# Splitting the first weight load by partitions, and four one-row copies for the result, in a decode kernel

## The chip, the cores and the metric

The kernel runs on one core of a Trainium2 chip. The metric is the time of one execution on the device, in microseconds. The kernel before was run three times: 203.63, 205.05 and 206.72 us, median 205.05. The profile was taken of an execution of 206.72 us, whose span from the first to the last instruction is 205.4 us.

## The reference

One token of a transformer block: LayerNorm, attention of 32 heads over a cache of 4096 keys and values, a residual, LayerNorm, a gated feed-forward with GELU, and a residual. All arrays are bf16.

```python
D, Hq, Sk, Dh, Df = 640, 32, 4096, 128, 1728
xn = layernorm(x)                                   # x: (1, 1, 640)
q = (xn @ wq).reshape(1, 1, 32, 128).transpose(0, 2, 1, 3)
scores = einsum("bhqd,bhkd->bhqk", q, k_cache) * Dh ** -0.5
o = einsum("bhqk,bhkd->bhqd", softmax(scores), v_cache)
h = x + o.transpose(0, 2, 1, 3).reshape(1, 1, 4096) @ wo
g, u = layernorm(h) @ w_gate, layernorm(h) @ w_up
return h + (gelu(g) * u) @ w_down
```

The inputs come to 84 MB, of which the two caches are 67 MB. Each is read once.

## The kernel before, in words

The program is written out by hand for five instruction queues: `sync` (SP, which issues nearly all DMAs), `gpsimd`, `vector`, `tensor` and `scalar`. A small class `Prog` collects operations per queue in program order, with the events that each one waits for, and `emit` writes them out with one semaphore per engine and one per DMA. `emit({"sync": 2})` places the first two operations of SP ahead of the barrier with which the program starts, so that they are issued before the other engines begin; the rest follows after it. Line 51 of the profile is the helper through which every DMA goes.

The loads form one long stream on SP's queue. First comes `wq` (L169), 640 x 4096, as one DMA into the SBUF tile `arena`: 128 partitions, on each five rows of the matrix, 40,960 bytes. Then come the caches in groups of four heads, `K` and `V` in turn (K0, V0, K1, K2, V1, K3, V2, ...), each 4 MB into one of three buffers `slot0` to `slot2` as 128 partitions of 32,768 bytes. `issue` sends the load of a slot when the group that held it has been consumed, so SP waits between loads on VectorE (for K) or TensorE (for V). After the last V group come `wo`, in three DMAs into `arena`, and then `w_gate`, `w_up` and `w_down` in several pieces into the slots.

The first use of `wq` is `q_proj` (L259), 40 matmuls that wait for the LayerNorm of x and for all of `wq`. Its result is copied to `qb` by VectorE (L263) and ScalarE (L264). For each K group VectorE multiplies the keys by q (L273), TensorE folds the products with an identity matrix (L281), VectorE reduces (L288), ScalarE takes the exponentials (L292), and TensorE multiplies by V (L310). In the feed-forward part `glu` (L417) forms gate and up, and `down` (L447) the last product.

`down` accumulates into four rows of one PSUM bank, `ps_d`, at partitions 0, 32, 64 and 96, 160 columns each, on top of the residual that four matmuls put there (L426). The last piece of `w_down` feeds one matmul for each quarter, `dn[0]` to `dn[3]`. Then ScalarE copies partitions 0 to 32 and VectorE partitions 64 to 96 into `out_row` (L460, L461), and one DMA stores rows 0, 32, 64 and 96 of `out_row` to the output.

Of the kernel before, what the change touches and what calls it, by code (L numbers as in the profile page):

```python
# [6 lines left out]
BF16 = mybir.dt.bfloat16  # L7
# [4 lines left out]
D = 640  # L12
# [89 lines left out]
def bass_sequential_preLN__gqa_block_cached__glu_gated_geglu__decode_kernel(nc, A_x, A_k_cache, A_v_cache, A_wq, A_wo, B_x, B_w_gate, B_w_up, B_w_down, out):  # L102
    sb = lambda name, shape, dt: nc.alloc_sbuf_tensor(name, shape, dt)
    SLOT = 10 * DF
    slots = [sb("slot%d" % i, [128, SLOT], BF16) for i in range(NSLOT)]
    arena = sb("arena", [128, 5 * 4096], BF16)
# [4 lines left out]
    RS = sb("RS", [128, H, 4], FP32)  # L111
    RT = sb("RT", [128, H], FP32)
    x_row = sb("x_row", [1, D], BF16)
    out_row = sb("out_row", [128, 160], BF16)
    xx = sb("xx", [128, 10], FP32)
    ln = sb("ln", [128, 8], FP32)
    xlnB = sb("xlnB", [128, 5, 32], BF16)
# [33 lines left out]
    ps_d = bank[3][:, 256:416]  # L151
# [8 lines left out]
    P = Prog(nc)  # L160
    V = lambda fn, *d: P.op("vector", fn, *d)
    A = lambda fn, *d: P.op("scalar", fn, *d)
    T = lambda fn, *d: P.op("tensor", fn, *d)
# [2 lines left out]

    A(lambda e: e.preload_act_table_set("natural_log_exp_and_others"))
    d_x = P.dma("scalar", x_row[:, :], A_x[0, :, :])
    d_wq = [P.dma("sync", arena[:, :], A_wq[:, :].rearrange("(p c) n -> p (c n)", c=5))]  # L169
    order = [("K", 0), ("V", 0), ("K", 1)]  # L170
    for G in range(1, NG - 1):
        order += [("K", G + 1), ("V", G)]
# [190 lines left out]
    for kind, G in order:  # L363
# [7 lines left out]
        if G == 4:  # L371
# [19 lines left out]
    d_wd = [P.dma("sync", wd_sb[:, 12, :], B_w_down[1536:1664, :], free[1]),  # L391
            P.dma("sync", wd_sb[:, 13, 0:320], B_w_down[1664:1728, :].rearrange("f (s n) -> (f s) n", s=2))]
# [49 lines left out]
    def down(ms, qs=range(4)):  # L442
        def fn(e):
            for m in ms:
                for q in qs:
                    h, n = (hm[:, m:m + 1], 160 * q) if m < 13 else (hm2[:, q // 2:q // 2 + 1], 160 * (q % 2))
                    i = e.matmul(ps_d[32 * q:32 * q + 1, 0:160], h, wd_sb[:, m, n:n + 160],  # L447
                                 start=False, stop=(m == 11))
            return i
        return fn  # L450
# [5 lines left out]
    T(down([13]), h2, d_wd[1])  # L456
    T(down(range(4, 8)), d_wd[3])
    T(down(range(8, 11)), d_wd[4])
    dn = {q: T(down([11], [q]), d_wd[5]) for q in range(4)}
    os = [A(lambda e: e.copy(out_row[0:33, :], ps_d[0:33, 0:160]), dn[1]),  # L460
          V(lambda e: e.tensor_copy(out_row[64:97, :], ps_d[64:97, 0:160]), dn[3])]  # L461
    d_out = P.dma("sync", out[0, :, :].rearrange("o (q n) -> (o q) n", q=4), out_row[::32, :], *os)
    P.op("sync", None, d_out)

    P.emit({"sync": 2})


# [26 lines left out]
```

## Time and profile before

| | before |
|---|---|
| median of three runs | 205.05 us (203.63 to 206.72) |
| profiled execution | 206.72 us, span 205.4 us |
| TensorE busy (matmul) | 118.7 us, 58% |
| VectorE busy | 100.8 us, 49% |
| ScalarE busy | 60.8 us, 30% |
| bytes read | 84.23 MB, 410 GB/s over the span |
| wq, issue to landing | 15.7 us |
| a K group, issue to landing (median of 8) | 21.9 us |
| mean granted TensorE clock | 0.838 |

The page cuts the span into 40 slices of about 5.1 us; a digit is the busy share of an engine in a slice in tenths. DMA is the mean busy share of 16 DMA engines. A line of the chain gives start, length and what ran, of the work that ended last. A line of the timeline gives start, length, engine, line, operation, tiles and shapes, and in brackets the idle time before it with what ended it. A line of the windows gives, after the stretch and its length, the busy time and instruction counts of TensorE's matmuls, its weight loads, VectorE, ScalarE and GpSimd, then the clock, the DMA share and the rate.

### The profile page before, as it was taken

The page shows a single profiled execution, that of the slowest core. Times are in us where ns is not written, and L with a number is a line of the kernel's source. Part 1 is how long each engine was busy: PE and PEld are TensorE (multiplying, and loading weights), DVE is VectorE, ACT ScalarE, POOL GpSimd, SP SyncE. Part 2 cuts the span into 40 slices and gives each one's busy share as a digit, 9 for nine tenths or more (in the row PEclk, how much of TensorE's full clock was granted, in tenths as well). Part 3 has the DMA queues.
Part 4 walks back from the last instruction along what each step waited for, and adds up shares of the span by engine and source line. Part 5 has one row for each costly group of instructions (what it writes and reads, how often), then busy time and mean ns, then how long its engine had stood idle before and what let it go on. Part 6 is the DMA issues. An engine that isn't in the chain of part 4 may idle for free.

```text
span 205.4 us, 2503 instructions
## 1 busy us (share of the span) xinstructions
PE 118.7 (58%) x1010; PEld 58.5 (28%) x1010; DVE 100.8 (49%) x105; ACT 60.8 (30%) x272; POOL 5.0 (2%) x14
## 2 busy tenths in 40 slices
PE   0107059438549777830957198539835787267494
PEld 0103023113213242410314033213322253167383
DVE  3201088427977869603791587187708940100221
ACT  2101005610662563630056136403640561100100
POOL 7100000000000000000000000000000000000000
PEclk9999758996985999996699969966996999955555
DMA  9999999999999999999999999999999999999970
GB/s 335 423 429 440 408 421 466 440 405 421 442 460 415 408 361 421 460 423 415 440 434 440 418 440 429 440 428 421 434 450 408 415 424 431 414 430 417 410 302 15
DMA packets 4341, 84.39 MB, mean 411 GB/s; under 512 B 489, under 2 KB 874, under 8 KB 1514
## 3 DMA queue, kind: packets, MB, share of 16 engines
q1 hardware_dynamic: 4328, 84.23, 96.4%
q8 instruction: 8, 0.13, 0.3%
q14 instruction: 3, 0.02, 0.0%
q10 hardware_dynamic: 2, 0.00, 0.0%
HBM read 84.23 MB, written 0.00 MB: 410 GB/s over the span
## 4 chain that ended last, share of the span: by engine, by line
DMA 63%; PE 17%; DVE 13%; issue 3%; SPq 3%
DMA slot<-in_A_k_cache_dram 41%; PE bank L281 12%; DVE prod L273 11%; DMA slot<-in_B_w_down_dram 11%; DMA slot<-in_A_v_cache_dram 11%; PE bank L310 3%; SPq L51 3%; DVE sc L288 1%; PE bank L319 1%; PE bank L447 0%; DVE out_row L461 0%; PE bank L330 0%; DVE RT L329 0%
## 5 line engine op out<-in xcount | busy, mean ns | idle before, releaser
L281 PE MATMUL bank<-prod,id_b 128*128 128x512 bf16 x256 | 73.5, 446 | 54.0 <-DVE prod L273 54.0
L273 DVE TENSOR_TENSOR prod<-slot,qb 128x4096 bf16<-128x4096 bf16 x32 | 72.4, 2284 | 33.8 <-DMA slot<-in_A_k_cache_dram 33.8
L292 ACT ACTIVATE p_bd<-sc,zero_t 32x32 bf16<-32x32 f32 x128 | 46.4, 362 | 87.7 <-DVE sc L288 86.5
L281 PEld LDWEIGHTS bank<-prod,id_b 128*128 128x128 bf16 x256 | 26.5, 112 | 101.1 <-DVE prod L273 66.6
L288 DVE TENSOR_REDUCE sc<-bank 128x32 f32<-128x512 f32 x32 | 22.0, 687 | 20.1 <-PE bank L281 20.1
L292 ACT ACTIVATION_READ_ACCUMULATOR p_bd<-sc,zero_t 32x1 f32 x128 | 23.5, 184 | 0.0
L310 PE MATMUL bank<-slot,p_bd 128*16 128x512 bf16 x256 | 17.3, 380 | 3.4 <-ACT p_bd L292 2.5
L310 PEld LDWEIGHTS bank<-slot,p_bd 128*16 128x16 bf16 x256 | 9.4, 89 | 7.6 <-ACT p_bd L292 3.0
L348 PE MATMUL bank<-aP,arena 128*128 128x1 bf16 x160 | 6.7, 178 | 5.3 <-DMA arena<-in_A_wo_dram 5.3
L319 PE MATMUL bank<-po_sb,hs 128*16 128x128 f32 x64 | 8.4, 274 | 1.1 <-ACT po_sb L314 1.1
L417 PE MATMUL bank<-hlnT,slot 128*128 128x1 bf16 (+1 forms) x140 | 6.7, 176 | 3.0 <-DMA slot<-in_B_w_gate_dram 3.0
L259 PE MATMUL bank<-arena,xlnB 128*32 128x512 bf16 x40 | 4.0, 578 | 7.3 <-DMA arena<-in_A_wq_dram 7.3
L348 PEld LDWEIGHTS bank<-aP,arena 128*128 128x128 bf16 x160 | 6.6, 131 | 5.5 <-DMA arena<-in_A_wo_dram 4.1
L314 ACT COPY po_sb<-bank 128x512 f32<-128x512 f32 x8 | 4.7, 585 | 9.9 <-PE bank L310 9.9
L417 PEld LDWEIGHTS bank<-hlnT,slot 128*128 128x128 bf16 (+1 forms) x140 | 6.3, 118 | 3.9 <-DVE hX L407 3.1
L244 ACT ACTIVATE ln<-ln,eps_t 128x1 f32<-128x1 f32 x2 | 0.6, 294 | 22.0 <-DVE ln L242 22.0
L319 PEld LDWEIGHTS bank<-po_sb,hs 128*16 128x16 f32 x64 | 5.6, 96 | 4.4 <-issue 2.1
L404 DVE TENSOR_TENSOR hT<-xx,bank 128x5 f32<-128x5 f32 x1 | 0.2, 161 | 11.7 <-PE bank L348 11.7
L263 DVE CAST qb<-bank 128x512 bf16<-128x512 f32 x1 | 0.7, 692 | 9.7 <-PE bank L259 9.7
L233 PE MATMUL bank<-one_bf,x_row 1*128 1x1 bf16 x5 | 0.4, 177 | 7.1 <-DMA x_row<-in_A_x_dram 7.1
L259 PEld LDWEIGHTS bank<-arena,xlnB 128*32 128x32 bf16 x40 | 1.6, 138 | 9.3 <-issue 9.3
L334 DVE TENSOR_SCALAR aT<-bank,rz 16x128 bf16<-16x128 f32 x2 | 0.7, 339 | 6.3 <-PE bank L319 6.3
(65 smaller groups left out, 25.7 us busy)
## 6 DMA issues: line engine op xcount, KB each, us to landing
slot<-in_A_k_cache_dram SPq DMA_DIRECT2D x8, 4096.0 KB, 21.9
slot<-in_A_v_cache_dram SPq DMA_DIRECT2D x7, 4096.0 KB, 18.1
arena<-in_A_wq_dram SPq DMA_DIRECT2D x1, 5120.0 KB, 15.7
slot<-in_A_v_cache_dram SPq DMA_DIRECT2D x2, 2048.0 KB, 19.9
arena<-in_A_wo_dram SPq DMA_DIRECT2D x1, 2560.0 KB, 29.0
slot<-in_B_w_gate_dram SPq DMA_DIRECT2D x1, 2160.0 KB, 17.1
arena<-in_A_wo_dram SPq DMA_DIRECT2D x1, 1920.0 KB, 33.1
slot<-in_B_w_up_dram SPq DMA_DIRECT2D x1, 1296.0 KB, 19.7
```

The source lines that it names most:

```text
L51: ev = self.op(eng, lambda e: e.dma_start(out, in_), *deps, dma=True)
L259: i = e.matmul(ps_q[hf][32 * j:32 * j + 32, :], xlnB[:, c, :], wq_j[:, c, j, 4 * hf:4 * hf + 4, :], start=(c == 0), stop=(c == 4))
L263: qa = V(lambda e: e.tensor_copy(qb[:, 0:4, :].rearrange("p g d -> p (g d)"), ps_q[0][:, :]), qd)
L273: m = V(lambda e: e.tensor_tensor(out=prod[:, s % 4, :, :], in0=kt[:, 32 * u:32 * u + 32, :], in1=qb[:, G, :].unsqueeze(1).to_broadcast([1 ...
L281: i = e.matmul(ps_f[s % 2][:, :], id_b[:, :], prod[:, s % 4, :, 16 * b:16 * b + 16], start=(b == 0), stop=(b == 7))
L288: reds[s] = V(lambda e: e.reduce_sum(sc[:, s % 4, :], ps_f[s % 2][:, :].rearrange("p (g d) -> p g d", d=16), axis=AX.X), folds[s], exps.ge ...
L292: x = A(lambda e, j=j: e.activation(p_bd[32 * j:32 * j + 32, G % 2, 32 * (s % 4):32 * (s % 4) + 32, j], sc[32 * j:32 * j + 32, s % 4, :], ...
L310: i = e.matmul(po[a:a + 16, :], p_bd[:, G % 2, 4 * b:4 * b + 4, :].rearrange("p g j -> p (g j)"), vt[:, 4 * b:4 * b + 4, :], start=(b < 4) ...
L314: evs[G] = A(lambda e: e.copy(po_sb[:, G % 2, :], po[:, :]), pvs[G], hds.get(G - 2))
L319: i = e.matmul(ps_a[0:16, 128 * (G // 4):128 * (G // 4) + 128], hs[:, r, 12 - 4 * g:28 - 4 * g], po_sb[:, G % 2, 128 * r:128 * r + 128], s ...
L348: r = e.matmul(ps_p[:, c:c + 1], wo_sb[:, t, i, c::5], aP[:, t, i:i + 1], start=(t == 0 and c == 0 and i == 0), stop=(t == 1 and i == 15), ...
L417: i = e.matmul(ps[0:128 if m < 13 else 64, m:m + 1], ws, hlnT[:, c:c + 1], start=(c == 0 and m == 0), stop=(c == 4), skip_group_check=True)
```

## The change

The load of `wq` becomes two DMAs, of partitions 0 to 15 and of partitions 16 to 127, with the same bytes in the same places. `q_proj` waits for both. Three operations of SP stand ahead of the starting barrier in place of two, so that both pieces and K0 do.

At the end, `out_row` is one row of 640 in place of 160 columns on 128 partitions. The last four matmuls run in the order of quarters 0, 2, 1, 3. VectorE copies quarters 0 and 1 and ScalarE quarters 2 and 3, one row of 160 each, and the store is one row of 640. All else keeps its place on its engine; line numbers behind the change are one higher up to the last matmuls.

```diff
-    out_row = sb("out_row", [128, 160], BF16)
+    out_row = sb("out_row", [1, D], BF16)
...
-    d_wq = [P.dma("sync", arena[:, :], A_wq[:, :].rearrange("(p c) n -> p (c n)", c=5))]
+    wq_v = A_wq[:, :].rearrange("(p c) n -> p (c n)", c=5)
+    d_wq = [P.dma("sync", arena[lo:hi, :], wq_v[lo:hi, :]) for lo, hi in ((0, 16), (16, 128))]
...
-    dn = {q: T(down([11], [q]), d_wd[5]) for q in range(4)}
-    os = [A(lambda e: e.copy(out_row[0:33, :], ps_d[0:33, 0:160]), dn[1]),
-          V(lambda e: e.tensor_copy(out_row[64:97, :], ps_d[64:97, 0:160]), dn[3])]
-    d_out = P.dma("sync", out[0, :, :].rearrange("o (q n) -> (o q) n", q=4), out_row[::32, :], *os)
+    dn = {q: T(down([11], [q]), d_wd[5]) for q in (0, 2, 1, 3)}
+    os = [V(lambda e, q=q: e.tensor_copy(out_row[0:1, 160 * q:160 * q + 160], ps_d[32 * q:32 * q + 1, 0:160]), dn[q])
+          for q in range(2)]
+    os += [A(lambda e, q=q: e.copy(out_row[0:1, 160 * q:160 * q + 160], ps_d[32 * q:32 * q + 1, 0:160]), dn[q])
+           for q in range(2, 4)]
+    d_out = P.dma("sync", out[0, :, :], out_row[:, :], *os)
     P.op("sync", None, d_out)
...
-    P.emit({"sync": 2})
+    P.emit({"sync": 3})
```

## The prediction

> **What bounds the kernel now.** I read the page's slices first, then the DMA queues, the chain of work that ended last, windows over the first and the last microseconds, and the timeline of the end.
>
> ```profile
> DVE  3201088427977869603791587187708940100221
> DMA  9999999999999999999999999999999999999970
> GB/s 335 423 429 440 408 421 466 440 405 421 442 460 415 408 361 421 460 423 415 440 434 440 418 440 429 440 428 421 434 450 408 415 424 431 414 430 417 410 302 15
> ...
> q1 hardware_dynamic: 4328, 84.23, 96.4%
> ```
>
> The 16 DMA engines are full in 38 of 40 slices; no compute engine is. The queue line gives the price of a byte: 84.23 MB in 96.4% of 16 x 205.4 us is 26.6 GB/s for one DMA engine. A row of wq on one partition is 5 x 4096 bf16, 40,960 bytes, so it takes one engine 1.54 us, and the 128 rows over 16 engines take eight such turns, 12.3 us.
>
> The chain says the same (start, length, what):
>
> ```profile
> 1.64 43.14 DMA slot<-in_A_k_cache_dram
> ...
> 75.24 20.37 DMA slot<-in_A_k_cache_dram
> ...
> 112.88 21.58 DMA slot<-in_A_k_cache_dram
> ...
> 151.24 22.15 DMA slot<-in_A_v_cache_dram
> ...
> 180.28 22.17 DMA slot<-in_B_w_down_dram
> ...
> 203.27 0.33 DVE out_row L461
> ```
>
> Only 44.8 to 75.2 us is compute. The queue serves wq, K0, V0 and K1 in order before K1 lands at 44.78, so whatever delays wq delays everything.
>
> The windows show how the stream starts and dies out (length, busy us and instruction counts of five engines, TensorE clock, DMA share, GB/s):
>
> ```profile
> 0.00:5.00 5.00, 0.00 (x0) 0.00 (x0) 1.61 (x8) 1.28 (x1) 3.87 (x12) 1.00 0.91 328
> 5.00:10.00 5.00, 0.96 (x7) 0.77 (x7) 1.33 (x6) 0.59 (x2) 1.15 (x3) 1.00 1.04 451
> ...
> 198.50:199.00 0.50, 0.50 (x14) 0.48 (x13) 0.00 (x0) 0.00 (x0) 0.00 (x0) 0.50 0.57 225
> 199.00:199.50 0.50, 0.50 (x14) 0.49 (x14) 0.00 (x0) 0.00 (x0) 0.00 (x0) 0.50 0.38 149
> 199.50:200.00 0.50, 0.50 (x14) 0.47 (x13) 0.00 (x0) 0.00 (x0) 0.00 (x0) 0.50 0.22 87
> 200.00:200.50 0.50, 0.42 (x10) 0.32 (x7) 0.00 (x0) 0.00 (x0) 0.00 (x0) 0.50 0.12 49
> 200.50:202.30 1.80, 1.55 (x41) 1.26 (x41) 0.33 (x2) 0.00 (x0) 0.00 (x0) 0.50 0.06 26
> ```
>
> A share of 0.06 is one engine of 16: from 200.5 us a single laggard finishes, while half of the engines were done by about 199 (share 0.57, then 0.38). The laggard ends at 202.4, so a typical other engine may come about 3.4 us later at no cost.
>
> The end, from the timeline:
>
> ```profile
> 202.88 0.09 PEld L447 LDWEIGHTS bank<-slot,hm 128*1 128x1 bf16 x4 [0.16 <-DMA slot<-in_B_w_down_dram]
> 203.23 0.29 ACT L460 CAST out_row<-bank 33x160 bf16<-33x160 f32 x1 [5.58 <-PE bank L447]
> 203.27 0.33 DVE L461 CAST out_row<-bank 33x160 bf16<-33x160 f32 x1 [2.14 <-PE bank L447]
> 203.69 0.63 SPq L51 DMA_DIRECT2D out_dram<-out_row  x1
> ```
>
> The two copies run side by side behind the last four matmuls, which all wait for the last w_down piece.
>
> [...]
>
> **The change part by part.**
>
> 1. First piece of wq: 16 rows, one per engine. [...] the piece takes four turns, 4 x 1.54 = 6.2 us[...], where these 16 rows cost one turn, 1.54 us. No work hides it: the queue behind holds more loads of the same ring.
>
> 2. Second piece: 112 rows, seven per engine, at least 7 turns = 10.8 us. The sum of both is 11 turns against 8, so +3 turns = +4.6 us is the lower bound. What comes on top depends on which seven rows an engine gets, which nothing here shows. I take blocks of seven neighbouring rows (16 to 22, 23 to 29, and so on), the plainest division. [...] After K0, [...]the sixteen are late by 3 turns (two engines), 4 (one), 5 (nine), 6 (three) and 7 (one): 4.6, 6.2, 7.7, 9.2 and 10.8 us.
>
> 3. What of this reaches the end. Early landings need all 16 engines, so wq, K0 and K1 land up to 10.8 us later, and the compute from 44.8 to 75.2 moves with K1. At the end the latest counts: the laggard with its own delay (5 turns in 9 of 16 cases), or another engine with its delay less 3.4 us (10.8 - 3.4 = 7.4 at the most). So 7.7 us is what I take; ends 4.6 and 10.8. The later compute does not add to it: V2's load is issued at 70.55 with the engines still working off K3 until about 72, and the laggard longer, so issuing it some 10 us later while the engines run 7.7 late costs the early engines a pause that the laggard does not see. If that cover is missing, the 10.8 counts in full.
>
> 4. Start. A further issue of about 0.39 us stands on SP ahead of K0, and K0's and the barrier's end move by up to 0.45 us. K0 has 12 us of wq ahead of it; V0 and K1 lie further back. The x load on ACT, the LayerNorm and q's weights move as much, and they are ready at 10.1 us, before wq lands at 15.7. So nothing. A smaller first issue could start the engines sooner: the window 0 to 5 us moved 328 GB/s, 1.64 MB, which at 430 takes 3.8 us; of the 1.2 us lost about 1.0 lies before the first packet and stays. Between 0 and -0.3; I take 0.
>
> 5. End. Four copies of one row replace two of 33. A copy's 160 columns stay, so I keep 0.33 us on DVE and 0.29 on ACT, two after one another on each. The first of each follows the matmuls of quarters 0 and 2, now put first, about 0.05 us earlier than 203.23, and successive copies overlap by some 0.1: DVE ends near 203.2 + 0.33 + 0.23 = 203.76 where it ended at 203.60. +0.15. One row of 1,280 bytes instead of four of 320: the x load, of the same shape, took 0.50 us to issue against 0.63, and one engine carries it; -0.1 to +0.1. I take +0.1 together, ends -0.1 and +0.4. Nothing hides it; it is last in the chain.
>
> Sum: +7.7 + 0 + 0.1 = +7.8 us. The profiled execution took 206.72 us, 1.3 more than its span of 205.4; it would become 214.5. The median of the three runs is 205.05, so my forecast is 212.8.
>
> **The rivals.**
>
> - The 112 rows are spread without collisions[...]. Only the first piece costs: +4.6 + 0.1, 209.8 us. [...]
> - Not slower. Rows keep the engine of their partition[...] 205.05 + 0.1 = 205.1 us. It decides if the first five microseconds still move over 300 GB/s. [...]
> - Rows are dealt in turn[...]: 8 x 4 = 32 turns against 8, +24 turns = +37 us, 242 us. [...]
>
> A forecast within 2% (about what a measurement of this kernel can tell from no change) would need the delay below 4.1 us.
>
> **How the numbers follow.** Blocks[...] 0.58 (209.7 to 216.0, by points 2 and 3), clean spread 0.22, no effect 0.14, dealt in turn 0.06. The range takes in the first two with the ends of points 4 and 5 and leaves out the other two: 208.0 to 217.0. Slower by over 2% (above 209.15): 0.58 + 0.06 + 0.17 of the second = 0.81. Within 2%: 0.14 less 0.03 for a gain at the start or another that I have not seen, plus the 0.05 left of the second, 0.16. Faster: 0.03.
>
> **What would show it.** In the profile after: 1 to 7 us at some 105 GB/s instead of 430; q's first matmul (L259 before, 15.79 us) at 22 to 27 us; the first product of K0 (25.38 before) 7 to 11 us later; the slices full as before from there on; DVE's copies as two in a row. The forecast is wrong if the first window keeps its rate and wq lands by 17 us, or if wq lands after 35 us.

## The result, and the profile after

The changed kernel takes 215.63 us (median of six runs, 215.30 to 216.02) against 204.34 us for the kernel before (six runs, 203.34 to 206.72). The ratio is 1.0564, 95% interval 1.0519 to 1.0610: slower by 11.3 us. The forecast was 212.8 us in a range of 208 to 217, so the direction and the range held, and the size was short: +7.8 us forecast against +11.3. The range held in part by luck: it was reckoned from the first median, 205.05. From 204.34 the prediction's own worst case for the split, 10.8 us, and its 0.1 for the end give 215.2, less than was measured.

The profile shown before is of an execution that was 2.4 us over the median of before, so stages are compared below with the run `tail_only` (first experiment), which has the same end as the changed kernel and the whole load of wq.

From the page of the changed kernel and its view of the DMAs, the slices, the DMA queue and two lines of the DMA issues (issuing queue, count, size, us to landing):

```profile
DVE  3001001884397991875179257728842791000321
DMA  9989899999999999999999999999999999999993
GB/s 122 245 245 245 214 435 441 416 465 392 462 416 418 459 404 447 419 423 455 410 453 416 423 444 416 455 410 435 441 410 450 416 410 432 430 415 426 408 415 129
...
q1 hardware_dynamic: 4338, 84.23, 97.9%
...
arena<-in_A_wq_dram SPq DMA_DIRECT2D x1, 4480.0 KB, 27.2
...
arena<-in_A_wq_dram SPq DMA_DIRECT2D x1, 640.0 KB, 8.5
```

The DMA digits stay at 8 or 9 while the rate is 245 GB/s or less in the first five slices, some 27 us, and then back at 392 to 465 until the last slice. A packet that moves slowly counts as busy like a fast one, so the busy share alone hides the loss; the rate shows it. The same stretch in windows, which count a packet where it starts, so that a share can come out above 1 and a rate is rough while rows take several microseconds:

```profile
0.00:5.00 5.00, 0.00 (x0) 0.00 (x0) 1.61 (x8) 1.28 (x1) 3.41 (x11) 1.00 1.00 131
5.00:10.00 5.00, 0.00 (x0) 0.00 (x0) 0.29 (x1) 0.00 (x0) 1.61 (x4) 1.00 1.11 229
10.00:15.00 5.00, 0.00 (x0) 0.00 (x0) 0.00 (x0) 0.00 (x0) 0.00 (x0) 1.00 1.01 279
15.00:20.00 5.00, 0.95 (x7) 0.78 (x7) 1.15 (x5) 0.59 (x2) 0.00 (x0) 1.00 0.92 221
20.00:25.00 5.00, 0.00 (x0) 0.00 (x0) 0.00 (x0) 0.00 (x0) 0.00 (x0) 1.00 0.87 208
25.00:30.00 5.00, 2.18 (x24) 1.00 (x28) 0.00 (x0) 0.00 (x0) 0.00 (x0) 1.00 0.98 387
```

Timeline of the changed kernel: x's arrival, q's first matmul, K0's and K1's first products, gate's first matmul, and the end:

```profile
15.16 0.35 PE L234 MATMUL bank<-one_bf,x_row 1*128 1x1 bf16 x5 [15.16 <-DMA x_row<-in_A_x_dram]
...
27.82 4.46 PE L260 MATMUL bank<-arena,xlnB 128*32 128x512 bf16 x40 [11.26 <-DMA arena<-in_A_wq_dram]
...
37.43 4.49 DVE L274 TENSOR_TENSOR prod<-slot,qb 128x4096 bf16<-128x4096 bf16 x2 [4.41 <-DMA slot<-in_A_k_cache_dram]
...
56.82 4.49 DVE L274 TENSOR_TENSOR prod<-slot,qb 128x4096 bf16<-128x4096 bf16 x2 [5.04 <-DMA slot<-in_A_k_cache_dram]
...
202.01 3.33 PE L418 MATMUL bank<-hlnT,slot 128*128 128x1 bf16 x70 [2.97 <-DMA slot<-in_B_w_gate_dram]
...
211.84 0.09 PEld L448 LDWEIGHTS bank<-slot,hm 128*1 128x1 bf16 x4 [0.18 <-DMA slot<-in_B_w_down_dram]
212.18 0.66 DVE L461 CAST out_row<-bank 1x160 bf16<-1x160 f32 x2 [2.21 <-PE bank L448]
212.21 0.59 ACT L463 CAST out_row<-bank 1x160 bf16<-1x160 f32 x2 [5.70 <-PE bank L448]
212.89 0.31 SPq L51 DMA_DIRECT2D out_dram<-out_row  x1
```

The same lines in `tail_only`, with wq whole and the new end:

```profile
7.06 0.35 PE L233 MATMUL bank<-one_bf,x_row 1*128 1x1 bf16 x5 [7.06 <-DMA x_row<-in_A_x_dram]
...
15.42 4.46 PE L259 MATMUL bank<-arena,xlnB 128*32 128x512 bf16 x40 [6.94 <-DMA arena<-in_A_wq_dram]
...
25.00 4.50 DVE L273 TENSOR_TENSOR prod<-slot,qb 128x4096 bf16<-128x4096 bf16 x2 [4.38 <-DMA slot<-in_A_k_cache_dram]
...
44.42 4.50 DVE L273 TENSOR_TENSOR prod<-slot,qb 128x4096 bf16<-128x4096 bf16 x2 [5.35 <-DMA slot<-in_A_k_cache_dram]
...
190.19 3.33 PE L417 MATMUL bank<-hlnT,slot 128*128 128x1 bf16 x70 [2.94 <-DMA slot<-in_B_w_gate_dram]
```

wq lands 27.82 - 15.42 = 12.4 us late, K0 and K1 12.4 us late, gate's first matmul 11.8, and the span ends 214.1 - 202.2 = 11.9 us late. The delay arises while wq and the first rows of K0 load, and nearly all of it is still there at the end.

The traces also hold the start and the duration of every DMA packet, and a packet of 40,960 bytes is one row of wq. In `tail_only` the rows that start after the first 5 us take 1.51 us each. In the changed kernel the rows of the first piece run from 1.02 to 7.18 us. The other 112 take 1.94 to 3.77 us each, half of them more than 2.8, and the last ends at 26.80. Before the change as after it 16 rows are under way at nearly every moment from 2.5 us on; what grows is the time of a row.

### The profile page after: what moved, and what is told of

Read it like the earlier page. It is cut to its first block, busy times and chain, and to the rows that moved or that the text cites. A ratio compares the mean times of both kernels' runs of the same rounds, so it can differ in the third digit from the quotient of the medians.

```text
span 214.1 us, 2506 instructions
## 1 busy us (share of the span) xinstructions
PE 119.6 (56%) x1010; PEld 58.3 (27%) x1010; DVE 101.1 (47%) x106; ACT 61.1 (29%) x273; POOL 5.0 (2%) x14
## 4 chain that ended last, share of the span: by engine, by line
DMA 58%; DVE 19%; PE 14%; issue 4%; another core or an unknown queue 2%; SPq 2%
DMA slot<-in_A_k_cache_dram 37%; DVE prod L274 15%; DMA slot<-in_B_w_down_dram 10%; DMA slot<-in_A_v_cache_dram 10%; PE bank L282 9%; DVE sc L289 3%; PE bank L311 3%; SPq L51 2%; PE bank L320 1%; PE bank L448 0%; DVE out_row L461 0%; PE bank L331 0%; DVE RT L330 0%
## 5 line engine op out<-in xcount | busy, mean ns | idle before, releaser
L282 PE MATMUL bank<-prod,id_b 128*128 128x512 bf16 x256 | 72.5, 440 | 51.5 <-DVE prod L274 51.5
L282 PEld LDWEIGHTS bank<-prod,id_b 128*128 128x128 bf16 x256 | 26.0, 110 | 98.8 <-DVE prod L274 65.1
L311 PE MATMUL bank<-slot,p_bd 128*16 128x512 bf16 x256 | 18.8, 409 | 3.3 <-ACT p_bd L293 2.5
L260 PE MATMUL bank<-arena,xlnB 128*32 128x512 bf16 x40 | 4.5, 631 | 11.3 <-DMA arena<-in_A_wq_dram 11.3
L315 ACT COPY po_sb<-bank 128x512 f32<-128x512 f32 x8 | 4.7, 585 | 11.3 <-PE bank L311 11.3
L265 ACT CAST qb<-bank 128x512 bf16<-128x512 f32 x1 | 0.6, 585 | 14.7 <-PE bank L260 14.7
```

The lines of the kernel that those rows point to most:

```text
L260: i = e.matmul(ps_q[hf][32 * j:32 * j + 32, :], xlnB[:, c, :], wq_j[:, c, j, 4 * hf:4 * hf + 4, :], start=(c == 0), stop=(c == 4))
L282: i = e.matmul(ps_f[s % 2][:, :], id_b[:, :], prod[:, s % 4, :, 16 * b:16 * b + 16], start=(b == 0), stop=(b == 7))
L311: i = e.matmul(po[a:a + 16, :], p_bd[:, G % 2, 4 * b:4 * b + 4, :].rearrange("p g j -> p (g j)"), vt[:, 4 * b:4 * b + 4, :], start=(b < 4) ...
L315: evs[G] = A(lambda e: e.copy(po_sb[:, G % 2, :], po[:, :]), pvs[G], hds.get(G - 2))
```

## The experiments

**The two parts of the change, each by itself.** `tail_only` is the changed kernel with wq as one load, and with two operations ahead of the barrier again:

```diff
-    d_wq = [P.dma("sync", arena[lo:hi, :], wq_v[lo:hi, :]) for lo, hi in ((0, 16), (16, 128))]
+    d_wq = [P.dma("sync", arena[:, :], A_wq[:, :].rearrange("(p c) n -> p (c n)", c=5))]
```

> wq is one load again; the four one-row copies and the one-row store stay. [...] all of the loss is in the split, so this is within 0.4 us of before, and since the store was issued in 0.31 us in place of 0.63 in the profile after, rather 0.2 us faster (ratio 0.998 to 1.001). Rival (the end costs part of it): 1 us or more above before.

Measured: 203.22 us against 203.56, ratio 0.9982 (0.9957 to 1.0006). The new end costs nothing that shows; whether it gains a few tenths this measurement doesn't tell.

`split_only` is the kernel before with wq in the two pieces of the change:

> Only wq is split into rows 0 to 15 and 16 to 127; the end is that of before. [...] +11 to +12 us, ratio 1.054 to 1.060, the first product of K0 at 37.4 us as in the profile after. Rival (the end costs part): below 1.05.

Measured: 215.75 us against 203.56, ratio 1.0608 (1.0580 to 1.0637), with K0's first product at 37.64 us:

```profile
37.64 4.50 DVE L274 TENSOR_TENSOR prod<-slot,qb 128x4096 bf16<-128x4096 bf16 x2 [4.53 <-DMA slot<-in_A_k_cache_dram]
```

The ratio is a little above the expected 1.054 to 1.060. The whole loss is in the split.

**Pieces by columns in place of rows.** `split_cols` has as many loads and as small a first piece:

```diff
+    d_wq = [P.dma("sync", arena[:, lo:hi], wq_v[:, lo:hi]) for lo, hi in ((0, 2560), (2560, 20480))]
```

> wq is split by columns: 2560 of 20480 elements of every partition first, then the rest. The same number of loads, the same small first piece of 655 KB, the same place ahead of the barrier, but each piece on all 128 partitions. [...] no loss, 0 to +0.4 us, q's first matmul at 15.5 to 16.3 us. Rival (a second load or a small first piece starts the stream badly, whatever its partitions): wq lands several us late and the time is over 210 us.

Measured: 203.52 us against 203.56, ratio 1.0004 (0.9982 to 1.0027), with q's first matmul at 15.13 us:

```profile
15.13 4.46 PE L260 MATMUL bank<-arena,xlnB 128*32 128x512 bf16 x40 [5.90 <-DMA arena<-in_A_wq_dram]
```

So neither a second load nor a small first one costs anything as such; the division by partitions does. The cut by columns does not gain either.

**Each piece by itself, away from the start.** These kernels are the one before with a load more between wq and K0, part of wq again, into the tile `prod`, which VectorE first fills later; K0's first product waits for it too:

```diff
+    d_ex = P.dma("sync", prod[0:16, :, :, :].rearrange("p a b d -> p (a b d)")[:, 0:16384], wq_v[0:16, 0:16384])
```

The other three differ in the ranges `[0:16]` and `[0:16384]`: 128 rows of 2048 elements as the control for this one, rows 16 to 127 of 16384, and 128 rows of 14336 as the control for that.

> Control for the next run: wq whole, then one load more, 524 KB of wq again into the tile prod, as 4,096 bytes on each of 128 partitions; the result does not use it. By bytes alone, 524 KB at 26.6 GB/s on 16 engines, +1.2 us: K0's first product at 26.6 us where before has 25.4. Both theories expect this.

> The same 524 KB, but as 32,768 bytes on each of partitions 0 to 15; the result does not use it. It measures the first piece by itself, away from the start. [...] 4 x 1.23 = 4.9 us instead of 1.2, K0's first product at 29.5 to 30.5 us. Rival (the first piece was slow because the stream was starting): +1.2 us like its control.

> Control for the next run: wq whole, then 3.67 MB of it again into prod as 28,672 bytes on each of 128 partitions; the result does not use it. By bytes, 8 turns of 1.08 us: +8.6 us, K0's first product at 34.0 us.

> The same 3.67 MB as 32,768 bytes on each of partitions 16 to 127; the result does not use it. It measures the second piece by itself. Seven turns of 1.23 us if the rows are spread cleanly: 34.0 us, like its control. Blocks of seven rows with only the colliding engines slowed, as the prediction stepped them: the worst engine 3 to 4 turns late, K0's first product at 37 to 39 us. If all engines run at about half speed, as the windows of the profile after suggest (245 GB/s): 3.67 MB at 245 GB/s are 15 us, K0's first product at 40 to 41 us.

Windows from 13 to 18 us and K0's first product, with q's first matmul for the first two, for the small control, the 16 rows, the large control (K0's product alone) and the 112 rows, in this order:

```profile
13.00:18.00 5.00, 2.21 (x24) 1.00 (x28) 0.00 (x0) 0.00 (x0) 0.00 (x0) 1.00 0.98 415
15.79 4.46 PE L261 MATMUL bank<-arena,xlnB 128*32 128x512 bf16 x40 [6.06 <-DMA arena<-in_A_wq_dram]
26.65 4.49 DVE L275 TENSOR_TENSOR prod<-slot,qb 128x4096 bf16<-128x4096 bf16 x2 [5.66 <-DMA slot<-in_A_k_cache_dram]
```

```profile
13.00:18.00 5.00, 0.00 (x0) 0.00 (x0) 0.00 (x0) 0.00 (x0) 0.00 (x0) 1.00 1.10 159
18.91 4.12 PE L261 MATMUL bank<-arena,xlnB 128*32 128x512 bf16 x40 [9.04 <-DMA arena<-in_A_wq_dram]
31.29 4.49 DVE L275 TENSOR_TENSOR prod<-slot,qb 128x4096 bf16<-128x4096 bf16 x2 [7.51 <-DMA slot<-in_A_k_cache_dram]
```

```profile
33.57 4.49 DVE L275 TENSOR_TENSOR prod<-slot,qb 128x4096 bf16<-128x4096 bf16 x2 [13.12 <-DMA slot<-in_A_k_cache_dram]
```

```profile
13.00:18.00 5.00, 0.95 (x12) 0.49 (x16) 0.00 (x0) 0.00 (x0) 0.00 (x0) 1.00 1.00 257
41.28 4.49 DVE L275 TENSOR_TENSOR prod<-slot,qb 128x4096 bf16<-128x4096 bf16 x2 [19.04 <-DMA slot<-in_A_k_cache_dram]
```

The same 524 KB take 31.29 - 26.65 = 4.6 us longer on partitions 0 to 15 than on all 128, and 3.67 MB take 41.28 - 33.57 = 7.7 us longer on partitions 16 to 127. The times say 3.5 and 6.9 us (209.02 against 205.53; 218.77 against 211.86). So both pieces are slow by themselves, not because the stream was starting, and the second one more. They came later than the theories put them: the 16 rows 0.8 us past the 30.5 of four turns, the 112 rows 0.3 us past the 41 of all engines at half speed and 2.3 us past the 39 of the prediction's blocks. With the larger rows of wq, 40,960 bytes in place of 32,768, 4.6 and 7.7 would be 5.8 and 9.6 us, estimated in proportion to the bytes; that they came to 12.4 together I have not explained.

**16 rows on other partitions.** `extra_16_spread` loads as many rows of the same size onto every fourth partition from 32 to 92:

> As the run with 32,768 bytes on each of partitions 0 to 15, but on every fourth partition from 32 to 92[...]. The result does not use these rows. [...] one turn, K0's first product at 26.5 to 27.2 us like the control with 128 partitions (26.65). Rival (a load of 16 rows is slow as such, one row for an engine, whatever its partitions): 31.3 us as for partitions 0 to 15.

```profile
26.21 4.49 DVE L276 TENSOR_TENSOR prod<-slot,qb 128x4096 bf16<-128x4096 bf16 x2 [5.60 <-DMA slot<-in_A_k_cache_dram]
```

26.21 us, 0.3 below the stretch expected for one turn, and 5.1 us before the same load on partitions 0 to 15; the time is 204.68 us, ratio 1.0055 (1.0025 to 1.0085). In the packet records the 16 rows take 1.21 us each, like rows of K0, where on partitions 0 to 15 they take 3.1 to 4.7. Both runs read the same rows of wq from memory, so what is read is not the cause; what differs is the partitions written. Sixteen rows are not slow as such; on the sixteen neighbouring partitions 0 to 15 they are. This is the run that carries the direction of the prediction. It shows neither why neighbours are slow nor how far apart rows have to lie.

**How rows are divided.** `split_64` cuts wq at partition 64:

> wq is split into rows 0 to 63 and 64 to 127, in place of 16 and 112. It asks how a load's rows are divided among the 16 engines. Blocks of neighbouring rows: four rows each,[...] so 8 turns for each half, 16 in place of 8, +12.1 us, q's first matmul at 27.5 to 28.5 us, the time at 215 to 217 us. Rows kept with the engine of their partition: no loss, 203.5 us. Rows dealt in turn:[...] +36 us, 240 us.

Windows of this run, and q's first matmul:

```profile
7.00:13.00 6.00, 0.00 (x0) 0.00 (x0) 0.00 (x0) 0.00 (x0) 0.14 (x1) 1.00 1.07 219
13.00:20.00 7.00, 0.95 (x7) 0.77 (x7) 1.16 (x5) 0.59 (x2) 0.00 (x0) 1.00 0.94 199
20.00:26.00 6.00, 0.00 (x0) 0.00 (x0) 0.00 (x0) 0.00 (x0) 0.00 (x0) 1.00 1.00 205
28.35 3.79 PE L260 MATMUL bank<-arena,xlnB 128*32 128x512 bf16 x40 [11.81 <-DMA arena<-in_A_wq_dram]
```

216.67 us, ratio 1.0594 (1.0520 to 1.0668), and q's first matmul where blocks of neighbouring rows put it. The two other divisions, as priced, are out by more than 10 us. The rows of wq that start after 5 us take 2.97 to 3.21 us each, about two turns of 1.51. So on 64 neighbouring partitions every row took twice its time, with little loss besides. The run does not show blocks: any division by which each row takes two turns would give the same.

**Are all rows slow, or a few?** The 245 GB/s of the changed kernel suggest that all rows were slow, and not a few. `extra_pairs` puts four loads of 16 rows behind wq, on every seventh partition from 3, 4, 7 and 15; I took each to have one pair of rows that hold each other up, the collision of the expectations, and no run shows such a pair. `extra_free4` is the same on every fourth partition from 32, 33, 34 and 35; `extra_16_step7` is one load on every seventh partition from 11. These two I took to have no pair.

> Four loads of 16 rows of 32,768 bytes behind wq, on every seventh partition from 3, 4, 7 and 15[...]. The result does not use them. It asks whether a collision holds only the two engines that collide, or all. Only the two: the other engines go on, and the stretch from 15 to 20 us moves over 350 GB/s, with K0's first product late for the one engine that collides each time, at 34 to 36 us. All held[...]: 16 rows in two turns, 200 to 260 GB/s in that stretch, the first product at 34 to 36 us as well.

> Control for the run with pairs: four loads of 16 rows of 32,768 bytes behind wq again, on every fourth partition from 32, 33, 34 and 35[...]. The result does not use them. If the collisions made the run with pairs slow: four turns of 1.23 us, the stretch from 15 to 20 us moves over 400 GB/s, K0's first product at 29.8 to 30.6 us. If four loads of 16 rows behind one another are slow as such: 260 to 290 GB/s and 34 us, as with pairs.

> One load of 16 rows of 32,768 bytes on every seventh partition from 11[...]. The result does not use it. If a step of seven partitions does no harm by itself: K0's first product at 26.2 to 26.8 us, as with the step of four. If the odd step made the run with pairs slow: one load of it costs about a quarter of that run's 9 us, 27.4 us or later.

The stretch from 15 to 20 us and K0's first product of the three, in this order:

```profile
15.00:20.00 5.00, 3.46 (x36) 1.51 (x40) 0.00 (x0) 0.00 (x0) 0.00 (x0) 1.00 1.12 282
34.20 4.49 DVE L279 TENSOR_TENSOR prod<-slot,qb 128x4096 bf16<-128x4096 bf16 x2 [12.47 <-DMA slot<-in_A_k_cache_dram]
```

```profile
15.00:20.00 5.00, 3.81 (x40) 1.51 (x40) 0.68 (x1) 0.58 (x1) 0.00 (x0) 1.00 1.08 465
29.90 4.49 DVE L279 TENSOR_TENSOR prod<-slot,qb 128x4096 bf16<-128x4096 bf16 x2 [9.89 <-DMA slot<-in_A_k_cache_dram]
```

```profile
15.00:20.00 5.00, 3.60 (x36) 1.64 (x40) 0.00 (x0) 0.00 (x0) 0.00 (x0) 1.00 1.02 374
27.78 4.49 DVE L276 TENSOR_TENSOR prod<-slot,qb 128x4096 bf16<-128x4096 bf16 x2 [6.18 <-DMA slot<-in_A_k_cache_dram]
```

The times are 212.74, 209.15 and 206.48 us, of two runs each, where before had 203.51 beside the first and 204.14 beside the others; the ratios of the last two, 1.0254 (1.0132 to 1.0376) and 1.0123 (1.0045 to 1.0201), are not clear of 2%. In `extra_pairs` the rate falls to 282 GB/s, between the stretches that I gave for the two cases; in `extra_free4` it is 465. The packet records say more. In `extra_pairs` the first 64 packets of 32,768 bytes behind wq take 1.55 to 2.68 us, all of them; in `extra_free4` all 64 take 1.21. So the loss is not that of one pair: every row is slow.

The third run came out as its second alternative had it. One load in steps of seven, which I had taken to be free of pairs, lost about 1.1 us against the control of 26.65 (four times that is about the 4.3 us between 34.20 and 29.90), q's first matmul came at 16.40 us, and the first 16 packets of 32,768 bytes took 1.62 to 2.09 us. So the step of seven costs by itself, and the run with four such loads says nothing of pairs. Why one load in steps of seven costs more than its bytes, and one in steps of four from 32 does not (26.21 us), stays open.

## Why the prediction was right, and where it was short

- *Point 1, the first piece.* Right in kind and, in this kernel, in size: four turns, 6.2 us, forecast; its rows ran from 1.02 to 7.18 us, and it landed 8.5 us after its issue. The four turns were my estimate; nothing in the trace of before shows them. By itself, `extra_16` cost 4.6 us more than its control where three turns of 1.23 us, 3.7, were due.
- *Point 2, the second piece.* The step that was mis-sized. Its delays of 3 to 7 turns were my estimate, with no run behind it, and let a row that meets no other go in one turn of 1.54 us. No row of this piece went that fast: the shortest took 1.94 us, half took more than 2.8, and the piece ended 19.6 us behind the last row of the first (7.18 to 26.80). Measured were 12.4 us for both pieces, 8.1 turns, where the estimate gave 3 to 7, 5 for most. That this piece is slow by itself is shown by `extra_112`, 7.7 us behind its control. What holds all its rows is the point left open above, and the blocks of seven neighbouring rows, on which the estimate rests, are not shown.
- *Point 3, what reaches the end.* It followed from point 2 that engines would differ, that the laggard would most likely be one of the nine with 5 turns, and that 7.7 of the 10.8 us would count. No such spread is seen: the third sixteen of K0's rows start within 1.2 us of one another (1.0 in `tail_only`), where delays of 4.6 to 10.8 us were forecast, and K0, K1 and the end are all 11.8 to 12.4 us late. The cover that I named, engines that may come 3.4 us later at no cost, was worth at most 0.6. The prediction's "the 10.8 counts in full" was the nearer case. Its reading that only 44.8 to 75.2 us of the chain is compute was wrong: 95.6 to 112.9 and 134.5 to 150.9 us are as well. The estimate did not rest on it, since the DMA digits stay at 9 there.
- *Point 4, the start.* Half right. The barrier and K0's issue moved by 0.45 us and cost nothing. But x moved by far more than that: its 1,280 bytes arrived at 15.16 us in place of 7.06. With wq cut by columns they arrived at 7.82, so it is the crowded rows that delayed them. The LayerNorm's result was ready at 18.2, still ahead of wq at 27.8; with wq on time it would have been late.
- *Point 5, the end.* Forecast +0.1. From the last weight load of `down` to the end of the span it is 214.1 - 211.84 = 2.26 us against 205.4 - 202.88 = 2.52 before. The copies on VectorE took 0.66 us in place of 0.33, where 0.56 was forecast, and the store's issue 0.31 in place of 0.63, where I had expected 0.50. The ratio of `tail_only` has no difference outside its interval.
- *The rivals.* Rows that stay with their engine at no loss, and rows dealt in turn at the price given, are both ruled out by `split_64` (216.67 us where they had 203.5 and 240); the clean spread by `extra_112` (K0's first product at 41.28 us where it had 34.0).
- *The signs.* Neither sign of being wrong appeared. But two of the others were passed: q's first matmul at 27.82 us where 22 to 27 was forecast, and K0's first product 12.1 us later than in the trace of before (25.38) where 7 to 11 was. The rate from 0 to 5 us, 131 GB/s, fits the forecast of some 105 from 1 to 7 us only roughly.

## What to carry to other kernels

In a kernel that lives on its DMA stream, if a load has to be cut, cut it along the columns and keep all 128 partitions in every piece: the cut by columns cost nothing (ratio 1.0004), the cuts at row 16 and at row 64 cost 12 and 13 us on 5.2 MB. In a profile look at the rate and not at the busy share, which reads 8 or 9 both at 122 to 245 GB/s and at 392 to 465. A delay at the head of such a stream arrived at its end nearly in full, 11.9 of 12.4 us.

## What the runs showed of the hardware that I had not expected

- A crowded load delays the one ahead of it: with the 16 rows of `extra_16` behind it, wq itself was late, q's first matmul at 18.91 us against 15.79 in its control. One row of wq took 3.67 us beside them, and the others after the first 5 us 1.51.
- A load of 1,280 bytes on another queue waited 8 us longer behind crowded rows (15.16 against 7.06 us).
- The store of one row of 1,280 bytes was issued in 0.31 us where four rows of 320 bytes took 0.63.
